# Regrouping copies in halves and one batch's value loads earlier, in a fused attention and gated feed-forward kernel

## The chip, the core and the metric

The kernel runs on one core of a Trainium2 chip. The metric is the device time of one execution in microseconds (us). Before the change the median of three runs is 412.39 us (412.38 to 412.73). The engines are named as in the profile: PE (TensorE), PEld (its weight loads), DVE (VectorE), ACT (ScalarE), POOL (GpSimd) and SP (SyncE). POOL and SP mainly issue DMAs here.

## The reference

Attention with a squared ReLU in place of the softmax, then a gated feed-forward layer:

```python
scores = q @ k.T / sqrt(64)
attn = maximum(scores, 0) ** 2 / 448
x = attn @ v                       # 8 batches, 12 heads, 448 rows, 64 columns
x = x by token                     # 3584 tokens of 768
out = (maximum(x @ w_gate, 0) * (x @ w_val)) @ w_out    # 768 -> 1536 -> 768
```

Inputs and output are float32; the kernel loads them into bf16 and accumulates in float32.

## The kernel before, in words

**Stages.** The eight batches are worked through as a pipeline. In turn b of the main loop (lines 740 to 785) PE computes the first projection of batch b-1, that is x @ w_gate and x @ w_val in twelve units of twelve steps (`gv_unit`, L304; ten units in turn 1), each step four 64x64 matmuls side by side. Between these steps stand the scores and value passes of batch b, and in turn 5 the first eleven of batch 6 as well. After turns 2 and 4 an `out_pair` (L357) computes the second projection of two batches, with sums and differences of blocks in place of some products. The last two batches have a first projection (`gv_pair`) and a second of the same kind at the end.

**Who does what for one tile.** A score tile goes into one of two PSUM pairs (L72). ACT takes the ReLU (r_sb, L234), DVE squares it into attn (L235). After seven tiles for each of three groups a value pass follows, whose result ACT (L268) and DVE (L269) copy to x, and DVE exchanges halves of partitions (L263). A unit of the first projection ends with a ReLU on ACT (g_sb, L322) and a product on DVE (hT, L323), which frees one of two accumulators for the unit after the next. For batches 6 and 7 the copies of the values are L278 to L281.

**Keys and queries.** The queries and keys of batches 2 to 7 are loaded into the same buffers kn and qn (`load_qk`, DMAs from POOL, L116). DVE regroups them by heads into kr and qr (`regroup`, L176, the copy at L179), and eight DMA transposes issued from SP (L186) bring them as kqT into one of two buffers. `hold(b)` (L676) is two tiny copies on POOL that read the last element of these transposes; POOL's queue, and so each load behind it, waits there.

**Order.** Every instruction is pinned to program order on its engine. The order comes from lists of events: an event is a unit, a step and a function, and `spread` (L690) calls it ahead of that step. `paced` places scores and value passes evenly over the turn. The regroupings, loads, holds and sums of weights are placed by hand in the lines 755 to 776. A place says where in each engine's queue the instructions stand; POOL and SP run ahead of PE as far as their waits allow.

**Weight sums.** `weight_sums(0)` and `(2)` (L343) are DVE operations on the rows of w_out, 128x2304 each (L347). They need the loads of w_out, which stand behind hold(2), and are used in the first `out_pair`.

**Stores.** `out_pair` issues its stores from POOL and SP (L411).

Of the kernel before, what the change touches and what calls it, by code (L numbers as in the profile page):

```python
# [16 lines left out]
def kernel(  # L17
# [22 lines left out]
    nc = tc.nc  # L40

    B, H, S, D = q.shape
# [25 lines left out]
    def pin(ins):  # L68
        return tc.keep_in_program_order(ins)
# [45 lines left out]
    def dma_in(o, i):  # L115
        pin(nc.gpsimd.dma_start(out=o, in_=i))  # L116
# [13 lines left out]
    def load_nat(dst, src, b, h0, h1):  # L130
        lo = src[b, h0:h1, 0:256, :].rearrange("h (j i) d -> j h i d", i=4)
        hi = src[b, h0:h1, 256:448, :].rearrange("h (j i) d -> j h i d", i=3)
        dma_in(dst[0:64, h0:h1, :, :], lo)
        dma_in(dst[64:128, h0:h1, 0:3, :], hi)

    def natural(b):

        return b if b < NB else 0

    def load_qk(b, h0=0, h1=H):  # L140
        load_nat(kn_b[natural(b)], k, b, h0, h1)
        load_nat(qn_b[natural(b)], q, b, h0, h1)

    def load_v(b):
        for c, p in HALVES:
            if b == 0:
                src = v[b].rearrange("(g c h) s d -> c h g s d", c=2, h=2)[c]
                dst = v_b[b % NB][p].rearrange("p (g h) i d -> p h g i d", h=2)
                parts = [(dst[:, h2], src[h2]) for h2 in range(2)]
            else:  # L150
                parts = [(v_b[b % NB][p], v[b, c * HP:c * HP + HP])]
            for dst, src in parts:
                dma_in(dst[:, :, 0:4, :], src[:, 0:256, :].rearrange("g (j i) d -> j g i d", i=4))
                dma_in(dst[:, :, 4:7, :], src[:, 256:448, :].rearrange("g (j i) d -> j g i d", i=3))
# [12 lines left out]
    def load_wo():  # L167
        for c in range(2):
            rows = moe_w_out[c * (d_ff // 2):(c + 1) * (d_ff // 2), :]
            dma_in(wo_sb[c], rows.rearrange("(kf p) m -> p kf m", p=128))  # L170
# [2 lines left out]

    T_b = [const.tile([128, 2, HP, S], BF16, name=f"kqT{i}") for i in range(NB)]

    def regroup(b, t):  # L176

        nat, grp = ((kn_b[natural(b)], kr), (qn_b[natural(b)], qr))[t]
        pin(nc.vector.tensor_copy(grp.rearrange("p i (h d) -> p i h d", d=D), nat.rearrange("p h i d -> p i h d")))  # L179

    def transpose_grouped(b, t):

        grp = (kr, qr)[t]
        for i in range(4):
            r = 128 if i < 3 else 64
            pin(nc.sync.dma_start_transpose(out=T_b[b % NB][:, t, :, i * 128:i * 128 + r], in_=grp[0:r, i, :]))  # L186

    def dma_transposes(b, t):
        regroup(b, t)
        transpose_grouped(b, t)  # L190

    def rotation(numbers):

# [97 lines left out]
    def quads(t):  # L291
        return [t[:, 2 * qd:2 * qd + 2, :] for qd in range(NQ)]

    def flat(t, n, c):

        names = " ".join("abcd"[:len(t.shape) - 1])
        return t.rearrange(f"p {names} -> p ({names})")[:, 0:n * c].rearrange("p (n c) -> p n c", c=c)

    def new_x(b):
        x = [xpool.tile([128, HP, S], BF16, name=f"x{n}") for n in range(2)]  # L300
        x_of[b] = [quads(t) for t in x]
        return x
# [40 lines left out]
    def weight_sums(n):  # L343

        o, a, b, op = ((T1, B12, B11, ALU.subtract), (B12, B22, B12, ALU.subtract),
                       (T2, B22, T1, ALU.subtract), (T4, B21, T2, ALU.subtract))[n]
        pin(nc.vector.tensor_tensor(o, a, b, op))  # L347
# [224 lines left out]
    def gv_units(b):  # L572
        b0 = b - b % 2
        if b == b0:
            hT_of[b0] = hpool.tile([128, KF, 2 * S], BF16, name="hT")
        return [gv_unit(b, mf, BEGUN, rotation((BEGUN_IN[mf],))) if b == 0 and mf < 2 else
                gv_unit(b, mf, BEGUN if mf == 0 else STRAIGHT, acc) for mf in range(KF)]
# [86 lines left out]
    def values_event(b, qd):  # L664
        return lambda: (values_by_parity if b >= B - 2 else values)(b, qd, sc_later())

    def transposes_event(b, qd):
        return lambda: transpose_quad(b, qd)
# [3 lines left out]
    def hold_unit(b, mf):  # L672

        pin(nc.gpsimd.tensor_copy(flag[:, 2:3], hT_of[b - b % 2][:, mf, b % 2 * S:b % 2 * S + 1]))

    def hold(b):  # L676

        for t in range(2):
            pin(nc.gpsimd.tensor_copy(flag[:, t:t + 1], T_b[b % NB][:, t, HP - 1, S - 1:S]))  # L679
# [23 lines left out]
        places = [at[int((i + 0.5) * len(at) / len(events))] for i in range(len(events))]  # L703
        return [(u, min(n, len(units[u]) - 4), e) for (u, n), e in zip(places, events)]

    def turned(b, *at):
        return [(u, n, lambda t=t: dma_transposes(b, t)) for t, (u, n) in enumerate(at)]

    def stream(b0, b1):

        e = []
        for b in range(b0, b1):
            for n in range(NT):
                if n % NC == 2 and (b, n) != (b0, 2):
                    vb, qd = (b, n // NC - 1) if n > NC else (b - 1, NQ - 1)
                    e.append((b, n, values_event(vb, qd), NC))
                e.append((b, n, scores_event(b, n), 1))
        return e

    def paced(units, first, behind, events):  # L720

        at = [(u, n) for u in range(len(units)) for n in range(len(units[u]))][first:behind]
        gaps = [{(1, 1): 1, (1, NC): 0.35, (NC, 1): 0.75}[a[3], b[3]] for a, b in zip(events, events[1:])]
        gap = len(at) / (sum(gaps) + 1)
        places, due = [], gap / 2
        for (*_, e, _), g in zip(events, gaps + [0]):
            u, n = at[int(due)]
            places.append((u, min(n, len(units[u]) - 4), e))
            due += g * gap
        return places  # L730
# [5 lines left out]
    units = gv_units(0)  # L736
# [3 lines left out]
    for b in range(1, B - 1):  # L740
        if b != B - 2:
            new_x(b)
        units = units[2:] if b == 1 else gv_units(b - 1)
        last = len(units) - 1
        if b < B - 3:
            first, behind = {1: (28, 109), 2: (40, 132)}.get(b, (0, 132))
            events = paced(units, first, behind, stream(b, b + 1))
            events.append((last, 8 if b == 1 else 5, values_event(b, NQ - 1)))
        else:
            todo = [e for e in attention if e[:2] <= ENDS[b]]  # L750
            del attention[:len(todo)]
            events = paced(units, 0, 144 if b == B - 3 else 132, todo)
            if b == B - 2:
                events.append((last, 5, values_event(B - 1, NQ - 1)))
        if b == 1:
            events += [(1, 2 + 4 * qd, transposes_event(1, qd)) for qd in range(NQ)]
            events += turned(2, (last - 3, 6), (last - 2, 6))
            events += [(last, 2, lambda: (hold(2), load_wo(), load_qk(3)))]
        elif b == 2:
            events += [(1, 1, lambda: load_v(3))]  # L760
            events += [(last - 2 + n, 6, lambda n=n: weight_sums(2 * n)) for n in range(2)]
            events += [(last - n, 9, lambda n=n: regroup(3, 1 - n)) for n in range(2)]
            events += [(last, 10, lambda: (transpose_grouped(3, 0), transpose_grouped(3, 1)))]
        elif b == 3:
            events += [(2, 1, lambda: (hold_unit(2, 1), hold(3), load_qk(4), load_v(4)))]
            events += turned(4, (6, 1), (7, 1)) + [(8, 2, lambda: (hold(4), load_qk(5)))]
        elif b == 4:
            events += turned(5, (3, 1), (4, 1)) + [(5, 2, lambda: (hold(5), load_qk(6), load_v(5)))]
        elif b == 5:
            events += turned(6, (1, 6), (2, 6)) + [(4, 1, lambda: (hold(6), load_v(6), load_qk(7)))]  # L770
            events += [(last - 3, 6, lambda: regroup(7, 0)), (last - 2, 3, lambda: regroup(7, 1))]
            events += [(last - 2, 6, lambda: (transpose_grouped(7, 0), transpose_grouped(7, 1)))]
            begun = flat(kn_b[1], 4, S)
            begun = x_of[B - 2] = [[begun[:, 2 * e:2 * e + 2, :]] for e in range(2)]
        elif b == 6:
            events += [(3, 1, lambda: (hold(7), load_v(7)))]
            new_x(b)
            for e in range(2):
                x_of[b][e][0] = begun[e][0]
            x_of[B - 1] = [quads(flat(t, HP, S)) for t in (kr, qr)]  # L780
        spread(units, events)
        if b == 2:
            out_pair(0, flat(kn_b[1], KH, S), [lambda: weight_sums(1), lambda: weight_sums(3)])
        elif b == 4:
            out_pair(2, flat(kn_b[1], KH, S))
# [45 lines left out]
```

## Time and profile before

| | |
|---|---|
| median of three runs | 412.39 us |
| the profiled execution | 411.69 us |
| its span | 409.9 us |
| mean TensorE clock granted | 0.993 |
| DMA moved | 44.17 MB |
| copies of L179 | 12, 0.95 to 0.96 us each |
| weight sums of L347 moved by the change | 2, 1.35 us each |

The span is what the profile covers of the execution. "Busy" counts the time in which an engine has an instruction under way; a matmul waiting in PE's own pipeline counts as busy. In timelines the bracket behind an instruction is the idle time of its engine just ahead of it and who ended it; "issue" means that the profile shows no releaser. The clock is the share of full TensorE speed that was granted.

### The profile page before, as it was taken

The numbers are of one execution on the slowest core, as the hardware profiler recorded it, in microseconds if no ns is written. First come the engines' busy times: TensorE is split into PE (matmuls) and PEld (weight loads), VectorE is DVE, ScalarE is ACT, GpSimd is POOL, SyncE is SP. The second block draws the span as 40 slices with busy tenths as digits, with TensorE's granted clock in tenths as the row PEclk, the third lists the DMA queues.
The fourth block names the chain that finished last, engine by engine and source line by source line (L and its number), as shares of the span: only waits on it lengthen the run. The fifth ranks groups of instructions, "written<-read, shape, count | busy, mean of one in ns | idle before, by whom it ended". The sixth has DMA issues, their size and how long they took to land.

```text
span 409.9 us, 16587 instructions
## 1 busy us (share of the span) xinstructions
PE 394.4 (96%) x7392; PEld 276.5 (67%) x7392; DVE 303.0 (74%) x520; ACT 244.1 (60%) x358; POOL 95.6 (23%) x164
## 2 busy tenths in 40 slices
PE   7899999999999999999999998899999999999994
PEld 4466666777776666666676686687677766777663
DVE  5885885589954786786833985888889969997651
ACT  4962984797334776877334888699973334444221
POOL 8834400610133502105034023020002230000230
PEclk9999999999999999999999999899999999999998
DMA  9999999699656994997927529960001350000144
GB/s 150 175 196 196 197 193 129 106 204 133 115 121 175 116 151 79 137 122 107 118 70 196 88 59 178 134 98 2 3 2 30 79 168 3 3 2 3 41 127 107
DMA packets 90984, 44.17 MB, mean 108 GB/s; under 512 B 55424, under 2 KB 89952, under 8 KB 90912
## 3 DMA queue, kind: packets, MB, share of 16 engines
q0 software_dynamic: 51136, 28.58, 49.0%
q1 hardware_dynamic: 39104, 13.99, 18.0%
q8 instruction: 58, 0.95, 1.0%
q10 hardware_dynamic: 672, 0.54, 0.6%
q14 instruction: 14, 0.11, 0.1%
HBM read 47.19 MB, written 11.01 MB: 142 GB/s over the span
## 4 chain that ended last, share of the span: by engine, by line
PE 69%; DMA 14%; DVE 7%; SPq 3%; issue 2%; POOL 2%; ACT 1%; DVEq 0%; POOLq 0%
PE ps L72 68%; DVE attn L235 4%; DMA wo<-in_moe_w_out_dram 4%; DMA qn<-in_q_dram 3%; DMA kn<-in_k_dram 3%; SPq L186 3%; DMA kqT<-qr 2%; DMA vn<-in_v_dram 2%; PE ps L210 1%; POOL kn L116 1%; DVE hT L323 1%; ACT r_sb L234 1%; POOL qn L116 1%; DVE x L642 1%; DVE kqT L211 0%
## 5 line engine op out<-in xcount | busy, mean ns | idle before, releaser
L72 PE MATMUL ps<-x,gv 64*64 64x448 bf16 x3552 | 204.6, 351 | 3.0 <-DVE hT L323 2.6
L72 PEld LDWEIGHTS <-gv 64*64 64x64 bf16 x4032 | 139.2, 107 | 58.3 <-issue 5.0
L234 ACT ACTIVATE r_sb<-ps 128x896 bf16<-128x896 f32 x167 | 147.8, 926 | 22.8 <-PE ps L72 19.4
L235 DVE TENSOR_TENSOR attn<-r_sb 128x896 bf16<-128x896 bf16 x167 | 102.3, 623 | 31.6 <-ACT r_sb L234 27.5
L72 PE MATMUL ps<-kqT 64*64 64x448 bf16 x672 | 67.8, 354 | 3.7 <-ACT r_sb L234 2.8
L72 PEld LDWEIGHTS <-hT 128*64 128x64 bf16 x1056 | 56.1, 110 | 20.9 <-issue 1.7
L411 POOL DMA_DIRECT2D out_dram<-attn x60 | 31.6, 531 | 163.5 <-DVE attn L401 131.9
L397 ACT ACTIVATE attn<-ps 128x384 f32<-128x384 f32 x64 | 28.9, 451 | 63.8 <-PE ps L72 63.2
L72 PE MATMUL ps<-wo,hT 128*64 128x384 bf16 (+1 forms) x720 | 53.9, 306 | 0.0
L323 DVE TENSOR_TENSOR hT<-ps,g_sb 128x448 bf16<-128x448 f32 x72 | 44.5, 619 | 9.3 <-ACT g_sb L322 8.8
L322 ACT ACTIVATE g_sb<-ps 128x448 bf16<-128x448 f32 x72 | 39.3, 547 | 18.5 <-PE ps L72 18.1
L401 DVE TENSOR_TENSOR attn<-ps,attn 128x384 f32<-128x384 f32 (+1 forms) x48 | 22.7, 503 | 32.1 <-ACT attn L397 18.1
L72 PEld LDWEIGHTS <-vn 64*64 64x64 bf16 (+1 forms) x840 | 30.8, 107 | 14.7 <-issue 3.9
L72 PEld LDWEIGHTS <-kqT 64*64 64x64 bf16 x672 | 27.2, 107 | 17.7 <-issue 7.5
L72 PE MATMUL ps<-attn,vn 64*64 64x448 bf16 x672 | 37.5, 350 | 1.0 <-issue 0.6
L515 ACT ACTIVATE kqT<-ps 128x896 f32<-128x896 f32 x18 | 16.5, 918 | 25.0 <-PE ps L72 25.0
L116 POOL DMA_DIRECT2D vn<-in_v_dram x36 | 23.7, 677 | 21.0 <-PE ps L72 5.8
L679 POOL COPY flag<-kqT 128x1 bf16<-128x1 bf16 x12 | 3.0, 252 | 101.6 <-DMA kqT<-kr 69.3
L72 PE MATMUL ps<-o_ring,hT 128*64 128x384 bf16 (+1 forms) x336 | 25.8, 306 | 0.1
L519 DVE TENSOR_TENSOR kqT<-ps,kqT 128x896 f32<-128x896 f32 x18 | 19.5, 1085 | 5.9 <-PE ps L72 4.2
L268 ACT ACTIVATE x<-ps 128x448 bf16<-128x448 f32 x15 | 8.2, 544 | 15.9 <-PE ps L72 15.9
L263 DVE COPY x<-x 64x896 bf16<-64x896 bf16 x36 | 14.4, 400 | 2.0
(104 smaller groups left out, 286.9 us busy)
## 6 DMA issues: line engine op xcount, KB each, us to landing
out_dram<-attn SPq DMA_DIRECT2D x48, 96.0 KB, 2.5
out_dram<-attn POOLq DMA_DIRECT2D x46, 96.0 KB, 2.3
kn<-in_k_dram POOLq DMA_DIRECT2D x7, 384.0 KB, 7.0
qn<-in_q_dram POOLq DMA_DIRECT2D x7, 384.0 KB, 9.2
vn<-in_v_dram POOLq DMA_DIRECT2D x14, 192.0 KB, 9.0
gv<-in_moe_w_gate_dram POOLq DMA_DIRECT2D x6, 384.0 KB, 11.3
gv<-in_moe_w_val_dram POOLq DMA_DIRECT2D x6, 384.0 KB, 10.9
wo<-in_moe_w_out_dram POOLq DMA_DIRECT2D x2, 1152.0 KB, 12.4
```

The lines of the kernel that those rows point to most:

```text
L72: pin(nc.tensor.matmul(o, lhsT=l, rhs=r, start=start, stop=stop, skip_group_check=True))
L116: pin(nc.gpsimd.dma_start(out=o, in_=i))
L234: pin(nc.scalar.activation(r, src, AF.Relu))
L235: pin(nc.vector.tensor_tensor(dst, r, r, ALU.mult))
L263: pin(nc.vector.tensor_copy(x1[p], x0[other]))
L322: pin(nc.scalar.activation(g_sb, o[0], AF.Relu, scale=float(out_scale)))
L323: pin(nc.vector.tensor_tensor(hT[:, mf, col:col + S], o[1], g_sb, ALU.mult))
L397: pin(nc.scalar.activation(out_of(t, r, c), bank(P, t), AF.Copy))
L401: pin(nc.vector.tensor_tensor(o, bank(Q, t), o, ALU.add))
L411: pin(engines[c].dma_start(out=rows[:, c0:c1, :], in_=src))
L515: pin(nc.scalar.activation(held(n, j), both(PQ[n][0]), AF.Copy))
L519: pin(nc.vector.tensor_tensor(k, both(PQ[n][1]), k, ALU.add))
```

## The change

`regroup` and `transpose_grouped` take a half h and treat two of the four groups of rows, so that each regrouping is two copies of 128x1536. `turned` places four pieces, keys' halves and queries' halves, each half with its two transposes, the second half five steps behind the first. `step` adds steps across the border of a unit. In the turns:

- turn 1 (batch 2): one step later, in halves.
- turn 2: the two weight sums three and two units sooner; batch 3's regroupings in halves at steps 3 and 8 of the last two units, keys first (they stood at step 9 of the last two units).
- turns 3 and 4 (batches 4 and 5): in halves from the same places; the holds and loads behind them two steps later in the lists.
- turn 4, new: the loads of batch 6's values at step 9 of the last unit, ahead of the second `out_pair`.
- turn 5: these loads no longer stand between hold(6) and the loads of batch 7's keys and queries; batch 7's regroupings move from unit 8, step 6 (keys) and unit 9, step 3 (queries) to units 9 and 10, steps 6 and 11; their transposes stand with them and no longer together at unit 9, step 6.

```diff
-    def regroup(b, t):
+    def regroup(b, t, h):
 
         nat, grp = ((kn_b[natural(b)], kr), (qn_b[natural(b)], qr))[t]
-        pin(nc.vector.tensor_copy(grp.rearrange("p i (h d) -> p i h d", d=D), nat.rearrange("p h i d -> p i h d")))
-
-    def transpose_grouped(b, t):
+        i = slice(2 * h, 2 * h + 2)
+        pin(nc.vector.tensor_copy(grp.rearrange("p i (h d) -> p i h d", d=D)[:, i],
+                                  nat.rearrange("p h i d -> p i h d")[:, i]))
+
+    def transpose_grouped(b, t, h):
 
         grp = (kr, qr)[t]
-        for i in range(4):
+        for i in (2 * h, 2 * h + 1):
...
-    def turned(b, *at):
-        return [(u, n, lambda t=t: dma_transposes(b, t)) for t, (u, n) in enumerate(at)]
+    def step(units, u, n, k):
+        at = len(units[0]) * u + n + k
+        return at // len(units[0]), at % len(units[0])
+
+    def turned(b, units, *at):
+
+        def piece(t, h):
+            regroup(b, t, h)
+            transpose_grouped(b, t, h)
+        return [(*step(units, u, n, 5 * h), lambda t=t, h=h: piece(t, h)) for t, (u, n) in enumerate(at) for h in range(2)]
...
-            events += turned(2, (last - 3, 6), (last - 2, 6))
+            events += turned(2, units, (last - 3, 7), (last - 2, 7))
...
-            events += [(last - 2 + n, 6, lambda n=n: weight_sums(2 * n)) for n in range(2)]
-            events += [(last - n, 9, lambda n=n: regroup(3, 1 - n)) for n in range(2)]
-            events += [(last, 10, lambda: (transpose_grouped(3, 0), transpose_grouped(3, 1)))]
+            events += [(last - 5 + 2 * n, 6, lambda n=n: weight_sums(2 * n)) for n in range(2)]
+            events += [(last - 1 + t, 3 + 5 * h, lambda t=t, h=h: regroup(3, t, h)) for t in range(2) for h in range(2)]
+            events += [(last, 10, lambda: [transpose_grouped(3, t, h) for t in range(2) for h in range(2)])]
...
-            events += turned(4, (6, 1), (7, 1)) + [(8, 2, lambda: (hold(4), load_qk(5)))]
+            events += turned(4, units, (6, 1), (7, 1)) + [(8, 4, lambda: (hold(4), load_qk(5)))]
...
-            events += turned(5, (3, 1), (4, 1)) + [(5, 2, lambda: (hold(5), load_qk(6), load_v(5)))]
+            events += turned(5, units, (3, 1), (4, 1)) + [(5, 4, lambda: (hold(5), load_qk(6), load_v(5))), (last, 9, lambda: load_v(6))]
...
-            events += turned(6, (1, 6), (2, 6)) + [(4, 1, lambda: (hold(6), load_v(6), load_qk(7)))]
-            events += [(last - 3, 6, lambda: regroup(7, 0)), (last - 2, 3, lambda: regroup(7, 1))]
-            events += [(last - 2, 6, lambda: (transpose_grouped(7, 0), transpose_grouped(7, 1)))]
+            events += turned(6, units, (1, 6), (2, 6)) + [(4, 1, lambda: (hold(6), load_qk(7)))]
+            events += turned(7, units, (last - 2, 6), (last - 1, 6))
```

More of the change, by code (lines that the diff above doesn't have):

```diff
@@ L174 @@
     T_b = [const.tile([128, 2, HP, S], BF16, name=f"kqT{i}") for i in range(NB)]
-    def regroup(b, t):
+    def regroup(b, t, h):
         nat, grp = ((kn_b[natural(b)], kr), (qn_b[natural(b)], qr))[t]
-        pin(nc.vector.tensor_copy(grp.rearrange("p i (h d) -> p i h d", d=D), nat.rearrange("p h i d -> p i h d")))
-    def transpose_grouped(b, t):
+        i = slice(2 * h, 2 * h + 2)
+        pin(nc.vector.tensor_copy(grp.rearrange("p i (h d) -> p i h d", d=D)[:, i],
+                                  nat.rearrange("p h i d -> p i h d")[:, i]))
+    def transpose_grouped(b, t, h):
         grp = (kr, qr)[t]
-        for i in range(4):
+        for i in (2 * h, 2 * h + 1):
             r = 128 if i < 3 else 64
             pin(nc.sync.dma_start_transpose(out=T_b[b % NB][:, t, :, i * 128:i * 128 + r], in_=grp[0:r, i, :]))
-    def dma_transposes(b, t):
-        regroup(b, t)
-        transpose_grouped(b, t)
     def rotation(numbers):
```

## The prediction

> **What bounds the kernel now.** I read the page's busy times first, then the idle pieces of PE in order of time, then windows of one microsecond around the largest piece, and last the DVE and POOL timelines there, to see who held whom.
>
> ```profile
> PE 394.4 (96%) x7392; PEld 276.5 (67%) x7392; DVE 303.0 (74%) x520; ACT 244.1 (60%) x358; POOL 95.6 (23%) x164
> ...
> PEclk9999999999999999999999999899999999999998
> ```
>
> PE is busy 96% of 409.9 us, and the change leaves its instructions alone: their order on PE, ACT and SP is the same in both programs, and only DVE's and POOL's change. So all that can be gained is time in which PE stands idle or runs at less than its full clock. The idle pieces from 25 us on are 0.24 (53.7), 0.63 (59.0), 0.57 (65.6), 0.27 (101.8), 2.61 (257.3), 0.46 (292.9) and 0.28 (396.7): 5.1 us. The only slice with a lower clock ahead of the end is the one around 257.
>
> The one-microsecond windows there (columns: stretch, length, PE, PEld, DVE, ACT and POOL busy with counts, PE clock, DMA share, GB/s):
>
> ```profile
> 253.00:254.00 1.00, 1.00 (x31) 0.80 (x24) 0.00 (x0) 0.96 (x2) 0.00 (x0) 1.00 1.52 184
> ...
> 255.00:256.00 1.00, 0.00 (x0) 0.00 (x0) 0.77 (x1) 0.47 (x2) 0.00 (x0) 1.00 1.45 199
> ...
> 257.00:258.00 1.00, 0.68 (x12) 0.51 (x15) 0.80 (x2) 0.00 (x0) 0.00 (x0) 0.76 1.72 191
> 258.00:259.00 1.00, 1.00 (x17) 0.62 (x13) 0.15 (x1) 0.10 (x1) 0.00 (x0) 0.50 0.83 129
> 259.00:260.00 1.00, 1.00 (x16) 0.71 (x12) 1.00 (x2) 0.81 (x1) 0.00 (x0) 0.50 0.85 177
> 260.00:261.00 1.00, 1.00 (x16) 0.66 (x12) 1.00 (x3) 0.24 (x1) 0.00 (x0) 0.53 0.87 197
> 261.00:262.00 1.00, 1.00 (x28) 0.81 (x23) 1.00 (x3) 0.98 (x2) 0.00 (x0) 1.00 0.40 97
> ```
>
> DVE falls silent first (253 to 254), then PE (255 to 256); when PE returns its clock is 0.50 for about 3.4 us, with 16 matmuls counted per microsecond instead of 28. Who made DVE wait is in the timeline (start, length, instruction, idle before):
>
> ```profile
> 243.34 0.19 POOL L679 COPY flag<-kqT 128x1 bf16<-128x1 bf16 x1 [8.10 <-DMA kqT<-qr]
> ...
> 243.89 2.68 POOL L116 DMA_DIRECT2D vn<-in_v_dram  x4 [0.37 <-issue]
> ...
> 246.52 1.55 POOL L116 DMA_DIRECT2D kn<-in_k_dram  x2
> ...
> 248.00 1.58 POOL L116 DMA_DIRECT2D qn<-in_q_dram  x2
> ...
> 251.16 0.79 DVE L263 COPY x<-x 64x896 bf16<-64x896 bf16 x2
> ...
> 255.23 0.96 DVE L179 COPY kr<-kn 128x3072 bf16<-128x3072 bf16 x1 [3.28 <-issue]
> ...
> 256.65 0.62 DVE L323 TENSOR_TENSOR hT<-ps,g_sb 128x448 bf16<-128x448 f32 x1
> ...
> 257.32 1.17 PE L72 MATMUL ps<-x,gv 64*64 64x448 bf16 x10 [2.61 <-DVE hT L323]
> ```
>
> DVE stands at the regrouping of batch 7's keys (L179), a copy of what the keys' loads bring (the view of the tile kn names it as the one who waited, 3.3 us). These were issued at 246.5 and 247.3, behind the four loads of batch 6's values (2.68 us of POOL), and land 7.0 and 7.9 us later, at 255.2. Queued behind that copy on DVE stands hT L323, which frees a PSUM bank for PE.
>
> **Part by part.**
>
> *Batch 6's values ahead, batch 7's regroupings later.* The four value loads go to POOL's queue ahead of the stores of the second projection. There they wait for PE's last reading of the buffer, batch 4's last value pass, which ends near 196.7. Behind them queue POOL's stores, the first at 204.65 and waiting for DVE then, so 8 us cover four issues of 2.7 us. The transfers before them end at 200.9 (GB/s falls from 143 to 12), and 0.69 MB at about 190 GB/s is 3.6 us: done by 204.5. Cost nothing; uncovered, it would be a store a few us later, and the buffers that the stores free are wanted only 20 us on.
>
> In the old place the keys' loads then go out at 243.9 and 244.7. For batch 5, loaded with no values ahead, keys landed 5.6 and 6.5 us and queries 7.7 and 8.5 us after their issue. So keys land by 251.2, queries (last issue about 246.2) by 254.7. The regroupings move from unit 8, step 6 and unit 9, step 3 to units 9 and 10, steps 6 and 11. Units 8 and 9 end at 251.8 and 254.9 (their g_sb), so DVE reaches the first key half near 254, the first query half near 257: 2.8 and 2.3 us to spare. Even with the loads where they were (255.2, 258.7) DVE would wait a microsecond or two, not 3.3. So the stall goes: 2.61 us idle, and of the clock 0.24 + 0.50 + 0.50 + 0.47 = 1.71. **-4.3 us.** As a check, 250 to 270 shows 330 matmuls and 225 to 245 shows 424; the missing 94 at 20/424 us each are 4.4 us.
>
> The clock may be weighed against a rule of the skill. The trace shows 0.50 right behind a gap of 2.61 us, and full clock 3.4 us after PE resumed. The Trainium skill, "TensorE: Matmul & The Clock Gate" (Part 1), says that the clock halves after at least one idle window of about 3.4 us and returns after about 3.4 us of work. The return agrees; the fall does not, as the gap here is shorter. By the letter of that rule the gap would not be the cause of the 1.71 us and only 2.61 would be gained here; the sum goes by the trace.
>
> *Batch 7's transposes.* They stay in SP's queue, eight in a row, 5.19 + 6.08 us now. Started at 254.5 instead of 256.3, they end near 266 and land by 270 (DMA kqT<-qr took 3.3 to 4.4 us). The first score of batch 7 has 42 others since batch 5's start ahead of it; it stands at 277.60 now and would stand at 273. Three us are left; values 7, held behind them, land near 276 and are wanted at 288.0 - 4.6 = 283.4.
>
> *Halves.* No half is in the trace. From the 64x896 copy (0.39 us) and the 128x3072 copy (0.955) the slope is 0.26 ns per element with 0.16 fixed, so a half of 1536 is about 0.56; the bounds are 0.48 (half, no fixed part) and 0.955. Twelve pairs add 12 x 0.16 = 1.9 us to a DVE that is busy 303 of 409.9, on no path except where PE waits for DVE. One such place: batch 2. Keys land at 55.24, the copy runs 55.37 to 56.33, and PE waits 0.63 us for x L269, which ends at 59.0. Now one attn is done ahead of the copy; behind it come half, attn, hT, half, attn, x instead of whole, attn, attn, hT, attn, x. One attn less (0.54 us per start) and 0.16 more: x ends about 0.4 earlier. **-0.4.** SP's first two transposes start about 0.45 us earlier and cover the wait for the second half, here and for batches 4 to 6; the weights' loads behind hold(2) come no later.
>
> *Two weight sums sooner.* They leave 96.4 and 99.8 for the places behind an L263 in unit 6 (about 87.1) and behind the first attn past unit 7's hT (about 92.1). The weights landed at 84.2 and 90.4, so 1.7 us are left for the second. Their gain: attn L235 at 101.11, for which PE waits 0.27 us, comes sooner. **-0.3.** Their cost: 1.26 us of DVE each in a stretch where DVE idles about 1.1 us between 88 and 93. Followed instruction by instruction, x L269 then ends at 95.6 instead of 94.9, and the score at 95.45 needs that bank: **+0.2** (from 0 to 0.8).
>
> *Batch 7's regroupings beside work.* In the stall they cost nothing of their own; now 4 x 0.56 us stand in units 9 and 10, which last 3.1 us each with about 2.3 us of DVE work. DVE falls about a microsecond behind. PE has two accumulators, so a lag below a unit is covered, but the value copies L279 follow: **+0.2** (from 0 to 1.5, were all lag beyond 0.75 us to reach PE).
>
> *The rest.* The loads of batches 5 and 6 move two steps later, behind hold(4) and hold(5), which wait for SP anyway: 0. The 0.57 at 65.6 has no releaser and the 0.46 at 292.9 comes from ACT's order, which is the same: 0.
>
> Sum: -4.3 - 0.4 - 0.3 + 0.2 + 0.2 = **-4.6 us**. The profiled execution took 411.69 us (span 409.9 and 1.8 around it), so 407.1 for its like; the median of the runs is 0.70 above it, so **407.8**.
>
> **Rivals.** (a) *DVE or ACT becomes the bound behind the stall.* Against: 225 to 245 has DVE 18.0 and ACT 17.9 of 20 us busy and PE still 19.9. For: after the stall DVE is full until 268. If 1 to 2.5 us come back as small waits: 408.8 to 410.3.
>
> (b) *The half clock is not the gap's doing* and is met elsewhere: only 2.61 + 0.3 is gained, 409.5. Against it: no other slice is low before the end. This is the result that the Trainium skill's rule above would have.
>
> (c) *Nothing moves*: hold(6) ends so much later that the queries still land 3 us behind DVE. Against: its transposes are SP-bound, 228.5 to 240.0, and start sooner. About 412.
>
> (d) *Slower: batch 7's transposes come late.* Four transposes took 8.74 us beside loads at 56.5, against 5.2 here. Eight at that pace from 255 end at 272.5 and land at 276.5; PE, which arrives at 273.0, would idle 3.5 us and lose 1.7 by the clock, all that was gained: 413.0, and 414 with one more microsecond. It decides from a landing past 273. Against: hold(7) keeps the loads behind them, and the value loads that shared the DMA are gone.
>
> (e) *More is gained*: in the runs without profile, 0.7 us longer, the stall may be longer too. 406.4 to 406.9.
>
> **Numbers.** Forecast (407.0 to 408.7): 0.65. (a) 0.13, (b) 0.06, (c) 0.05, (d) 0.06, (e) 0.05. A measurement of this kernel can tell about 0.2%, 0.8 us, from no change. Faster: 0.65 + 0.13 + 0.06 + 0.05 = 0.89; same 0.05; slower 0.06. The range leaves out (c), (d) and the tail of (a): 406.6 to 410.0.
>
> **What would show it.** Right: no idle piece over 0.5 us between 230 and 270, PEclk 1.00 there, the keys' loads 2.7 us behind the flag gone to 0.5; 59.0 and 101.8 shrunk; the first POOL store within 0.5 us of where it was. Wrong: a regrouping with an idle time "issue" over 1 us ahead of it; score waits on ACT or DVE spread over 255 to 275; PE waiting at batch 7's first score; the second weight sum waiting for wo.

## The result, and the profile after

The changed kernel takes 407.66 us (median of 4 runs, 406.69 to 408.46), the kernel before 412.38 us beside it (4 runs, 411.17 to 412.73): the ratio is 0.989 [0.9858, 0.9922], faster by 4.7 us. The prediction was 407.8. All ratios are worked out from the runs within 1.5% of the fastest of their kernel (414.94 and 413.21, named below, are not) and so differ a little from those of the medians. The profiled execution took 406.69 us, with a span of 404.9. Line numbers are now two or three lower, except the regrouping copy (L179, now L180); L277 is the DVE half of the value copies, L279 before.

The page after, busy times and granted clock:

```profile
PE 393.0 (97%) x7392; PEld 276.3 (68%) x7392; DVE 303.9 (75%) x532; ACT 244.3 (60%) x358; POOL 96.0 (24%) x164
...
PEclk9999999999999999999999999999999999999999
```

The count of matmuls is the same, PE is busy 1.4 us less, and the 8 in the clock's row is gone. DVE has twelve more instructions (the halves) and 0.9 us more work.

The windows around the old stall (columns as before):

```profile
250.00:270.00 20.00, 19.37 (x408) 15.24 (x404) 18.22 (x34) 18.00 (x26) 2.97 (x6) 1.00 0.41 75
...
259.00:260.00 1.00, 0.37 (x9) 0.14 (x7) 0.97 (x3) 0.57 (x1) 0.00 (x0) 1.00 0.60 93
```

The same 20 us now hold 408 matmuls, where there were 330, and the clock is 1.00 throughout. One gap is left, in 259 to 260. The timeline shows both why the old one is gone and where the new one comes from:

```profile
239.15 0.19 POOL L677 COPY flag<-kqT 128x1 bf16<-128x1 bf16 x1 [5.82 <-DMA kqT<-qr]
239.71 1.64 POOL L116 DMA_DIRECT2D kn<-in_k_dram  x2 [0.37 <-issue]
241.34 1.51 POOL L116 DMA_DIRECT2D qn<-in_q_dram  x2
...
253.42 0.55 DVE L180 COPY kr<-kn 128x1536 bf16<-128x1536 bf16 x1
...
255.96 0.55 DVE L180 COPY qr<-qn 128x1536 bf16<-128x1536 bf16 x1
...
258.50 1.27 DVE L277 TENSOR_SCALAR kn<-ps 64x448 bf16<-64x448 f32 x2
259.82 0.38 PE L72 MATMUL ps<-kqT 64*64 64x448 bf16 x2 [0.63 <-DVE kn L277]
```

The keys' loads stand right behind the flag, the tiny copy of hold(6) that waits for the transposes (0.56 us later; it was 3.18). Keys land by about 246.5 and queries by 250.6 (the loads' own times from issue to landing are 5.2 to 8.5 us), so all four half copies (the second halves at 254.43 and 256.96) run without a bracket: DVE no longer waits. But four of them now stand ahead of the value copies L277, whose PSUM pair the next score needs, and PE waits 0.63 us for these.

The moved value loads, on POOL:

```profile
194.76 1.98 POOL L116 DMA_DIRECT2D vn<-in_v_dram  x3 [2.36 <-PE ps L72]
197.43 0.66 POOL L116 DMA_DIRECT2D vn<-in_v_dram  x1 [0.68 <-DMA qn<-in_q_dram]
202.98 4.23 POOL L409 DMA_DIRECT2D out_dram<-attn  x8 [4.89 <-DVE attn L399]
```

They wait for PE's last reading of the buffer and are issued by 198.1. POOL then waits another 4.89 us for what it is to store, so they hold up nothing.

**Where the 5.0 us of the span went.** PE reaches its landmarks sooner by: first projection 0.31, first `out_pair` 1.69, second 1.68, batch 7's first score 5.13, last product 5.13. The start-up (0.31) is the same program in both kernels. Turns 1 and 2 bring 1.38: the pieces at 59.0 (0.63), 65.6 (0.57) and 101.8 (0.27) are gone. Turns 3 and 4, which also got halves, bring nothing. Turn 5 brings 3.45: the 4.3 of the stall, less the new wait of 0.63 and 0.24 that I did not place. Whatever follows brings nothing.

### The profile page after: what moved, and what is told of

It reads as the page before. It is cut to its first block, busy times and chain, and to the rows that moved or that the text cites. A ratio compares the mean times of both kernels' runs of the same rounds, so it can differ in the third digit from the quotient of the medians.

```text
span 404.9 us, 16604 instructions
## 1 busy us (share of the span) xinstructions
PE 393.0 (97%) x7392; PEld 276.3 (68%) x7392; DVE 303.9 (75%) x532; ACT 244.3 (60%) x358; POOL 96.0 (24%) x164
## 4 chain that ended last, share of the span: by engine, by line
PE 79%; DVE 7%; DMA 5%; ACT 3%; issue 2%; SPq 2%; POOL 0%; DVEq 0%; ACTq 0%; POOLq 0%
PE ps L72 78%; DVE attn L233 4%; DMA kn<-in_k_dram 3%; ACT r_sb L232 3%; SPq L409 2%; DMA qn<-in_q_dram 1%; PE ps L208 1%; DMA out_dram<-attn 1%; DVE x L640 1%; DVE attn L399 0%; DVE kqT L209 0%; DVE hT L321 0%; ACT g_sb L320 0%; DVE kr L180 0%; DVE qr L180 0%
```

## The experiments

My theory: the four value loads ahead of the keys' loads make DVE wait at the regrouping, PE starves behind it, and the half clock follows from PE's gap; taking the loads out of the way gives nearly the whole gain. Rivals: the gain comes from the later place of the regroupings, from the halves or from the weight sums; or the half clock has nothing to do with the gap. The runs were made on three chips; the kernel before took 411.39, 412.57 and 412.65 us there, and each ratio is against the kernel before on the same chip.

**The value loads alone** (kernel before, whole copies, all else in its old place):

```diff
-            events += turned(5, (3, 1), (4, 1)) + [(5, 2, lambda: (hold(5), load_qk(6), load_v(5)))]
+            events += turned(5, (3, 1), (4, 1)) + [(5, 2, lambda: (hold(5), load_qk(6), load_v(5))), (last, 9, lambda: load_v(6))]
...
-            events += turned(6, (1, 6), (2, 6)) + [(4, 1, lambda: (hold(6), load_v(6), load_qk(7)))]
+            events += turned(6, (1, 6), (2, 6)) + [(4, 1, lambda: (hold(6), load_qk(7)))]
```

> The kernel before with one edit: batch 6's value loads stand ahead of the second out_pair's stores; everything else, the regroupings of batch 7 too, as before. My theory (the stall at 257 is batch 7's keys landing late, and the value loads ahead of them are what makes them late): keys land about 5 to 7 us after their issue near 243.5, that is by 250.5, DVE reaches their regrouping near 252.0, so no idle time ahead of it and no stretch at clock 0.50: 4.0 to 4.3 us less than before, ratio about 0.990. Rival A (the later place of the regroupings is what does it): the stall stays, under 1 us is gained. Rival B (the half clock is not the gap's doing): 2.6 us are gained and a stretch at 0.50 stays.

Measured 407.43 (406.54 to 407.8), ratio 0.9898 [0.9862, 0.9934]. Its timeline:

```profile
242.22 1.74 POOL L116 DMA_DIRECT2D kn<-in_k_dram  x2 [0.31 <-DVE attn L235]
...
252.68 0.96 DVE L179 COPY kr<-kn 128x3072 bf16<-128x3072 bf16 x1
...
255.16 0.95 DVE L179 COPY qr<-qn 128x3072 bf16<-128x3072 bf16 x1
```

and its window over the old stall:

```profile
250.00:270.00 20.00, 20.00 (x424) 15.59 (x420) 18.30 (x33) 17.83 (x26) 1.47 (x4) 1.00 0.48 89
```

Both copies run without a wait and PE stands still for nothing in 20 us: 424 matmuls, as many as in the undisturbed 225 to 245 of before. This one edit gives the whole gain that these measurements can tell. The pieces at 59.08 (0.63) and 101.87 (0.27) are still in its profile, as they should be.

**The later place alone** (loads in the old order, whole copies):

```diff
-            events += [(last - 3, 6, lambda: regroup(7, 0)), (last - 2, 3, lambda: regroup(7, 1))]
-            events += [(last - 2, 6, lambda: (transpose_grouped(7, 0), transpose_grouped(7, 1)))]
+            events += turned(7, (last - 2, 6), (last - 1, 6))
```

> The kernel before with one edit: batch 7's regroupings and their transposes stand in units 9 and 10, step 6 (whole copies), the loads as before. My theory as put on record: even then DVE would wait a microsecond or two, not 3.3; keys land at 255.2, DVE is there near 254; queries land at 258.7, DVE is there near 257.5. PE has an accumulator to spare, so PE idles 0 to 1 us: 3.0 to 4.3 us less than before, ratio 0.990 to 0.993. Rival A (only the loads' order counts, the wait just moves with the place): within 1 us of before.

Measured 410.53 (407.15 to 414.94), ratio 0.9962 [0.993, 0.9995]: 1.6 us by the ratio, not 3.0 or more. The expectation failed. The profiled execution took 407.15, the least of its runs. No copy waits there, and PE idles only for the value copies L279 (0.49 us at 260.07). Two more profiles of the same kernel follow.

> The kernel with only the later place of batch 7's regroupings, once more for a second profile: its twelve times went from 407.15 to 414.94 and its first profile, at 407.15, showed no wait. My theory: its gain hangs on when the loads land, which differs between executions; in a longer execution DVE idles ahead of a copy of kr or qr near 255, with PE idle behind it. Rival: no wait there in a longer execution either, so that the spread comes from elsewhere.

> The kernel with only the later place of batch 7's regroupings, for a third profile. My theory: in a longer execution DVE idles ahead of a copy of kr or qr near 255. Rival: it does not, and the spread comes from elsewhere.

The first of them (410.9 us) has DVE waiting 1.26 us for the queries and PE idle 1.85 us at 263.52, with the clock at 1.00. The second (413.67 us), its timeline:

```profile
261.13 0.96 DVE L179 COPY qr<-qn 128x3072 bf16<-128x3072 bf16 x1 [1.40 <-issue]
...
263.61 1.27 DVE L279 TENSOR_SCALAR kn<-ps 64x448 bf16<-64x448 f32 x2
...
264.93 0.38 PE L72 MATMUL ps<-kqT 64*64 64x448 bf16 x2 [1.98 <-DVE kn L279]
```

and its windows behind that gap:

```profile
266.00:267.00 1.00, 1.00 (x16) 0.72 (x12) 0.93 (x3) 0.70 (x2) 0.00 (x0) 0.50 0.48 105
...
270.00:271.00 1.00, 1.00 (x31) 0.76 (x23) 0.63 (x1) 1.00 (x3) 0.38 (x1) 1.00 0.01 0
```

DVE's wait has shrunk to 1.3 or 1.4 us, but PE's gap hardly has: the place only hands it from hT to the value copies L279, and no second buffer covers those. In this execution the flag came at 245.63, after POOL had waited 8.01 us for the queries' transposes. In the execution of 407.15 it came at 239.82, after 5.58 us. The queries landed near 255.3, 259.7 and 261.1 in the three profiles, and DVE waited for them 0, 1.26 and 1.40 us. With the later place alone, what is gained hangs on when the loads land.

**The kernel before, a second profile**, to learn whether the stall of the first is typical.

> The kernel before itself, for a second profile. My theory: DVE waits for batch 7's keys or queries again and PE idles 1.5 to 3 us near 257, but the sizes differ; where no single gap reaches about 2.6 us the clock stays at 1.00. If the stall is not there, the gain hangs on chance.

410.47 us: DVE waits 2.21 us at 254.25 (keys) and 1.04 at 257.85 (queries), and PE is idle 1.54 and 1.10 us, both at hT:

```profile
256.33 0.76 PE L72 MATMUL ps<-x,gv 64*64 64x448 bf16 x10 [1.54 <-DVE hT L323]
...
260.46 0.38 PE L72 MATMUL ps<-x,gv 64*64 64x448 bf16 x2 [1.10 <-DVE hT L323]
```

The clock stays at 1.00. So the stall is there again at 2.64 us of idle PE, in two pieces; the 1.71 us of lost clock are not.

**The values behind the keys and queries** (kernel before, loads still in turn 5):

```diff
-            events += turned(6, (1, 6), (2, 6)) + [(4, 1, lambda: (hold(6), load_v(6), load_qk(7)))]
+            events += turned(6, (1, 6), (2, 6)) + [(4, 1, lambda: (hold(6), load_qk(7), load_v(6)))]
```

> The kernel before with one edit: batch 6's value loads stand in the same event, but behind batch 7's key and query loads instead of ahead of them. It tells the order on POOL's queue from the earlier place ahead of the stores. My theory (the keys are late because the values are ahead of them): keys land 5 to 6 us after their issue and no copy of batch 7 waits; the values now land last, where the queries landed before, near 257.5, and PE's first value pass of batch 6 would stand near 257.5 without the stall, so 0 to 1.5 us are lost there: 2.8 to 4.3 us less than before. Rival (only the place ahead of the stores, with the DMA queue empty at hold(6), brings the gain): under 2 us less.

Measured 408.89 (406.86 to 413.21), ratio 0.993 [0.9884, 0.9976]: 2.9 us, within the expectation, but the interval (1.0 to 4.8 us) leaves room for the rival's "under 2 us", so the profile has to decide. The profiled execution took 407.57 us; its timeline:

```profile
243.72 1.54 POOL L116 DMA_DIRECT2D kn<-in_k_dram  x2 [0.37 <-DVE hT L323]
245.23 1.52 POOL L116 DMA_DIRECT2D qn<-in_q_dram  x2
246.70 2.69 POOL L116 DMA_DIRECT2D vn<-in_v_dram  x4
...
252.18 0.96 DVE L179 COPY kr<-kn 128x3072 bf16<-128x3072 bf16 x1
...
254.66 0.95 DVE L179 COPY qr<-qn 128x3072 bf16<-128x3072 bf16 x1
```

The same bytes at nearly the same time, in another order, and the stall is gone, though the flag came at 243.16, as late as in the first profile of before (243.34). So it is the order behind the values that held DVE, and the place ahead of the stores is one way to change it. The order costs twice: with the four value loads ahead, the keys' loads go out 2.7 us later, and they land 6.4 to 9.0 us after their issue in the seven profiles with that order, 4.9 to 7.0 here. The place ahead of the stores may be the steadier way: the runs in the ratio here reach 411.8, those of the loads alone end at 407.8; but those are six runs, on another chip. The values now land late (8.9 to 9.9 us after issue), and batch 6's value pass at 257.55 took 1.81 us where it takes 1.52 with the loads alone. That this is what spreads the runs was not shown.

**Halves alone** (the changed kernel, with the loads, batch 7's places and the weight sums put back as before):

```diff
-            events += [(last - 5 + 2 * n, 6, lambda n=n: weight_sums(2 * n)) for n in range(2)]
+            events += [(last - 2 + n, 6, lambda n=n: weight_sums(2 * n)) for n in range(2)]
...
-            events += turned(5, units, (3, 1), (4, 1)) + [(5, 4, lambda: (hold(5), load_qk(6), load_v(5))), (last, 9, lambda: load_v(6))]
+            events += turned(5, units, (3, 1), (4, 1)) + [(5, 4, lambda: (hold(5), load_qk(6), load_v(5)))]
...
-            events += turned(6, units, (1, 6), (2, 6)) + [(4, 1, lambda: (hold(6), load_qk(7)))]
-            events += turned(7, units, (last - 2, 6), (last - 1, 6))
+            events += turned(6, units, (1, 6), (2, 6)) + [(4, 1, lambda: (hold(6), load_v(6), load_qk(7)))]
+            events += [(last - 3, 6, lambda: [regroup(7, 0, h) for h in range(2)]),
+                       (last - 2, 3, lambda: [regroup(7, 1, h) for h in range(2)])]
+            events += [(last - 2, 6, lambda: [transpose_grouped(7, t, h) for t in range(2) for h in range(2)])]
```

> The kernel before with the regroupings of batches 2 to 6 in halves at the changed kernel's places; batch 7's two halves back to back in the old place, the value loads and the weight sums as before. My theory: the idle piece at 59.0 (0.63 us) goes, as in the changed kernel, and the stall at 257 stays at 2.6 us with its slow clock: 0.4 to 0.7 us less, 0.9985. The piece of 0.57 us at 65.6 that went too with the change has no releaser in the profile: if it goes here, it hangs on the halves of batch 2, else it is chance. Rival: the halves' extra time on DVE (1.9 us in all) shows as waits, 0 to 1 us more than before.

411.1 (408.61 to 413.83), ratio 0.9988 [0.996, 1.0017]: no difference that can be told. In its profile the stall is back, smaller than expected (1.62 us at 261.17, clock 1.00). The piece at 59 did not go, and one old wait has grown:

```profile
56.28 0.56 DVE L180 COPY kr<-kn 128x1536 bf16<-128x1536 bf16 x1 [0.46 <-DMA kn<-in_k_dram]
...
59.50 0.38 PE L72 MATMUL ps<-kqT 64*64 64x448 bf16 x2 [0.55 <-DVE x L267]
...
99.74 0.55 DVE L180 COPY kr<-kn 128x1536 bf16<-128x1536 bf16 x1
...
100.75 1.35 DVE L345 TENSOR_TENSOR o_ring<-wo,qn 128x2304 bf16<-128x2304 bf16 x1
102.01 0.62 DVE L233 TENSOR_TENSOR attn<-r_sb 128x896 bf16<-128x896 bf16 x1
```

At 59, batch 2's keys landed late and DVE waited 0.46 us for them, so 0.55 us of PE's idle time are left with halves: this part of the expectation failed. The piece at 65.6 is there too (0.56 at 66.04), so the halves do not remove it. Batch 3's first half copy now stands at step 3, ahead of the weight sum that still has its late place, and PE waits 0.73 us for the attn behind both, where it was 0.27. The two edits belong together.

**Weight sums alone** (kernel before):

```diff
-            events += [(last - 2 + n, 6, lambda n=n: weight_sums(2 * n)) for n in range(2)]
+            events += [(last - 5 + 2 * n, 6, lambda n=n: weight_sums(2 * n)) for n in range(2)]
```

> The kernel before with one edit: the two weight sums three and two units sooner. My theory: the idle piece of 0.27 us at 101.8 goes and no wait of PE comes in its place near 95, as the changed kernel showed none: 0.2 to 0.3 us less, which a measurement can hardly tell from no change; the pieces at 59.0 and 257 stay. Rival (the price of 0.2 on record, a score waiting for x L269 near 95): a piece of about 0.2 us there, nothing gained.

412.13 (408.88 to 414.49), ratio 1.0009 [0.9976, 1.0042]: no difference that can be told, as 0.3 us is below what these runs resolve. In the profile the piece at 101.8 is gone and no score waits near 95. Batch 2's keys landed late here (DVE waits 2.12 us for them), and the piece at 59 has grown to two, 1.05 at 59.08 and 0.63 at 61.22. In the stall PE is idle 0.79 us up to 257.88 and 1.99 us up to 262.90, 2.78 in all, and the clock stays at 1.00; the last section comes back to that.

**The changed kernel with whole copies** (each at its first half's place, batch 3's too, all else as changed):

```diff
-        i = slice(2 * h, 2 * h + 2)
-        pin(nc.vector.tensor_copy(grp.rearrange("p i (h d) -> p i h d", d=D)[:, i],
-                                  nat.rearrange("p h i d -> p i h d")[:, i]))
+        if h == 0:
+            pin(nc.vector.tensor_copy(grp.rearrange("p i (h d) -> p i h d", d=D), nat.rearrange("p h i d -> p i h d")))
...
-        return [(*step(units, u, n, 5 * h), lambda t=t, h=h: piece(t, h)) for t, (u, n) in enumerate(at) for h in range(2)]
+        return [(*step(units, u, n, 0), lambda t=t, h=h: piece(t, h)) for t, (u, n) in enumerate(at) for h in range(2)]
```

> The changed kernel with whole copies: each regrouping is one copy of 128x3072 at the place of its first half, its four transposes behind it; loads, places and weight sums as changed. My theory: the stall stays gone (the loads do that), what is lost against the changed kernel is at most the 0.6 us of the piece at 59.0, and some of it comes back since DVE does 1.9 us less: 0 to 0.6 us slower than the changed kernel. Rival (the halves carry a good part of the gain): over 1 us slower.

407.86 (407.27 to 409.94), ratio 0.9892 [0.9856, 0.9929]. **The changed kernel again**, on the same chip:

> The changed kernel itself, for a narrower interval on the same chip as the three others and for a second profile. My theory: as measured first, ratio 0.988 to 0.990, with the new piece of PE idle time near 260 behind the value copies (0.63 us in the first profile, DVE kn L277) there again, since it comes from DVE's order; the piece of 0.57 us at 65.6 may or may not be there, since it came and went in kernels that differ nowhere near it. If the 0.63 is not there, it was chance too.

408.94 (406.8 to 410.32), ratio 0.9902 [0.9871, 0.9934], where 0.988 to 0.990 was expected. Whole copies are as fast. At 58.55 their profile has a piece of 0.33 us, where before had 0.63 and the changed kernel has none. That does not split the gain between halves and place, since the piece hangs on when batch 2's keys land: it is 0.37 in the second profile of before and 0.55 with halves alone. The repeat has the new wait again:

```profile
261.37 0.38 PE L72 MATMUL ps<-kqT 64*64 64x448 bf16 x2 [0.62 <-DVE kn L277]
```

So 0.62 to 0.63 us belong to the order on DVE, not to one execution. Whole copies have it too (0.58 at 261.84, and 0.49 with the later place alone): it comes with the place, not with the halves. The 0.57 us piece at 65.6 is the contrary: in the repeat it is back at 64.87 (0.54, "issue"), so its absence after was chance.

**Batch 7's regroupings one unit sooner** (changed kernel), to get rid of that wait:

```diff
-            events += turned(7, units, (last - 2, 6), (last - 1, 6))
+            events += turned(7, units, (last - 3, 6), (last - 2, 6))
```

> The changed kernel with batch 7's four pieces one unit sooner (units 8 and 9, steps 6 and 11). Keys and queries landed by 246.5 and 250.6 in the changed kernel's profile, so neither waits there; the pieces leave the stretch ahead of the value copies of batch 6. My theory (the wait of 0.63 us near 260 is DVE lag from four halves packed into units 9 and 10): it shrinks to under 0.2, 0.3 to 0.6 us less than the changed kernel. Rival (the wait comes from the value copies' own place): it stays, no difference.

407.24 (406.35 to 409.25), ratio 0.9873 [0.9835, 0.991]. The window of the profile:

```profile
250.00:270.00 20.00, 19.98 (x416) 15.90 (x412) 18.15 (x35) 17.82 (x26) 0.35 (x2) 1.00 0.77 124
```

The wait near 260 is gone, and PE has no idle piece of 0.2 us or more from 135 to 290, though the flag came as late as 245.26. This is the lowest median of all, faster than the kernel before; the intervals do not tell it from the changed kernel.

**Gaps made on purpose** (changed kernel, with 16 to 24 DVE writes of a tile that nothing reads, in turns 2 to 5; it adds work and leaves none out):

```diff
+        late = {2: 16, 3: 20, 4: 24, 5: 20}.get(b)
+        if late:
+            events.append((4, 6, lambda: [pin(nc.vector.memset(blank, 0.0)) for _ in range(late)]))
```

> The changed kernel with DVE held up on purpose in turns 2 to 5: 16, 20, 24 and 20 memsets of a tile that nothing reads again, at unit 4, step 6. Each should make PE idle for some time, none of it over a missing load. My theory (the clock falls because PE stood idle, and only past some length): behind gaps under about 2 us, as with the 1.62 and 1.99 us met in two runs so far, the clock stays at 1.00; behind a gap of 2.6 us or more it is 0.50 for about 3.4 us, as at 257 before the change. Rival (the half clock there had another cause): gaps of 2.6 us and more here leave the clock at 1.00.

One run, 435.08 us. PE's gaps are 3.65, 4.86, 6.93 and 4.05 us, and a stretch at 0.50 stands behind each. The second of them:

```profile
148.00:149.00 1.00, 0.00 (x0) 0.00 (x0) 0.73 (x3) 0.00 (x0) 0.00 (x0) 1.00 1.49 194
...
150.00:151.00 1.00, 0.00 (x0) 0.00 (x0) 0.66 (x4) 0.00 (x0) 0.00 (x0) 0.50 1.49 193
...
153.00:154.00 1.00, 1.00 (x17) 0.59 (x12) 1.00 (x3) 0.26 (x1) 0.00 (x0) 0.50 0.00 0
...
157.00:158.00 1.00, 1.00 (x29) 0.69 (x21) 0.01 (x1) 0.86 (x1) 0.00 (x0) 1.00 0.08 16
```

PE stopped near 146.8; the clock falls while it still stands, and is back 4.8 us after it resumes at 151.67. So the gap makes the half clock, wherever in the program it is put.

## Why the prediction was right, point by point

- **The stall, -4.3.** Right in cause and, for the profiled pair, in size: 2.61 idle and 1.71 of clock are both gone, and the loads alone give a ratio of 0.9898. But 4.3 was one execution's stall. In the second profile of before the idle part is the same (2.64), with weight sums alone it is 2.78, and in both the clock's part is nothing. Sized over executions it lies between 2.6 and 4.3, and the medians do not contradict that: 4.0 for the loads alone, 3.6 and 4.7 for the whole change.
- **Batch 7's regroupings beside work, +0.2 (0 to 1.5).** Mis-sized: 0.63 and 0.62 in two profiles. The way was named, the value copies. What the estimate missed is that two accumulators cover the lag of hT but nothing covers L277.
- **Halves, -0.4.** The piece of 0.63 at 59.0 is gone in both profiles of the changed kernel, but 0.55 of it is left with halves alone, where the keys landed later: the estimate took their landing as fixed. A half took 0.55 us (0.56 expected). In time halves show nothing alone (0.9988 [0.996, 1.0017]).
- **Weight sums, -0.3 and +0.2.** The 0.27 at 101.8 is gone; the price did not appear, no wait near 95. The sums ran at 85.64 and 90.70, neither waiting for wo. In time they show nothing alone either.
- **The rest, 0.** The 0.57 at 65.6 and the start-up's 0.31 are gone from the profile after, by chance. Without these 0.88 the profile's -5.0 is -4.1, against the -4.6 predicted. The new wait cost 0.43 more than put down, but the piece at 59.0 gave 0.23 more and the price of the sums 0.2, which cancels it; the 0.5 us that are missing lie in small pieces that I did not place (0.24 of them in turn 5).
- **The total.** 407.66 against 407.8 is closer than these terms deserve, so part of it is luck: in the profiled pair chance added 0.88 us, and a stall with its clock part, which some four in ten executions have (last section), had been taken for typical. Measured again on another chip the changed kernel took 408.94, 3.6 us below the kernel before there, and the intervals are about 0.3% to each side, not the 0.2% that I had thought could be told.
- **Margins.** Keys and queries landed 7 and 5 us ahead of DVE, not 2.8 and 2.3: the flag came at 239.15, since the queries' transposes landed 5.8 us behind the keys' (8.1 before). That is not the change's doing; two profiles of one kernel above have 5.8 and 8.0.
- **The first store within 0.5 us of its place.** It came at 202.98 instead of 204.65, with PE, which is 1.68 us sooner there.
- **"Even with the loads where they were DVE would wait a microsecond or two".** DVE did (1.26, 1.40); the 3.0 us or more that I then expected of the place alone was wrong, as PE's gap stayed near 1.9 us.

**The rivals.** (a) DVE and ACT are full from 250 to 270 (18.2 and 18.0) and give back 0.63, below the 1 to 2.5 asked for. (c) falls with the loads alone. (d) was never near: the last transposes landed at 267.34, batch 7's first score came at 272.47, 5.1 us later. (b) falls in its first half, since gaps made on purpose bring the half clock. The Trainium skill's rule in "TensorE: Matmul & The Clock Gate" (Part 1), an idle window of about 3.4 us, does not tell when if it is read as an unbroken gap: gaps of 2.61 (before) and 1.98 us were followed by 0.50, gaps of 1.99, 1.85, 1.62 and 1.54 were not. As the length of a window it agrees, 3.41 us here; the last section shows from the profiles what decides. The clock was back 3.6 us after PE resumed; 3.4 is how long it stood at 0.50. (e) needs 406.4 to 406.9, and neither median of the changed kernel (407.66, 408.94) is there.

## What to carry to other kernels

When an engine idles "<-issue" at a copy of loaded data, look at what stands ahead of that load in the issuing queue: loads that are wanted later can be put behind it or into an earlier slot of the same queue, and that was worth 0.7% and 1.0% here. Moving the consumer later instead trades the wait for one at the next result without a second buffer. Size such a stall from two or three executions, the half clock behind it above all, before it goes into a sum.

## What the hardware showed beyond that

- **The clock is set every 3.41 us, by how long PE idled since it was last set.** In the run with gaps the clock fell at 84.80, 149.65, 194.02, 265.70 and, behind the end of PE's work, 432.96. These falls stand 19, 13, 21 and 49 times 3.413 us apart, and each stretch at 0.50 between them lasted that once or twice. In the kernel before, the falls at 257.52 and 407.70 stand 44 times apart. So the fall at the end of a profile shows where the borders lie in all of it, and PE's idle time can be counted from border to border:

| profile | border to border | PE idle | clock behind it |
|---|---|---|---|
| before | 254.11 to 257.52 | 2.61 | 0.50 |
| later place, third profile | 262.31 to 265.72 | 1.98 | 0.50 |
| gaps | 149.65 to 153.06 | 2.02 | 0.50 |
| changed kernel, its end | 397.93 to 401.35 | 1.91 | 1.00 |
| later place, second profile | 260.00 to 263.41 | 1.74 | 1.00 |
| weight sums alone | 258.60 to 262.02 | 1.11 | 1.00 |
| weight sums alone | 262.02 to 265.43 | 0.88 | 1.00 |

Two rows of the view of windows, the third profile of the later place and then the first row of the weight sums (PE's busy time stands behind the length):

```profile
262.31:265.72 3.41, 1.43 (x33) 0.80 (x28) 3.32 (x8) 1.37 (x3) 0.28 (x1) 1.00 0.62 140
258.60:262.02 3.42, 2.31 (x52) 1.55 (x41) 1.74 (x3) 2.42 (x4) 0.00 (x0) 1.00 0.80 131
```

In the fourteen profiles no such stretch with 1.98 us idle or more is followed by the full clock, and none with 1.91 or less by 0.50. That is why a gap of 1.98 us cost the clock and one of 1.99 did not: a border at 262.02 cut the second in two. The borders lie elsewhere in each execution, so the same gap costs the clock in one and not in the next.
- **How often the stall cost the clock.** In the thirteen profiles without added gaps the mean clock of the execution is 0.993 for the two with a stretch at 0.50 ahead of the end, and 0.996 to 1.000 for the others. At 0.994 or below are 23 of the 56 runs of the kernel before that stand beside the experiments, and none of the 31 runs of kernels with the value loads moved ahead of the stores (lowest 0.996).
- **The spread is smaller without the race for the loads.** On its three chips the kernel before ran from 409.1 to 414.1, 410.3 to 415.1 and 408.5 to 414.2 us (runs in the ratios). With the value loads moved the runs lie from 406.5 to 407.8 (loads alone), 406.8 to 410.3 (changed kernel again) and 406.4 to 409.3 (one unit sooner). POOL waited 8.1 and 5.7 us for the same four transposes in two profiles of before, and 5.6, 5.8 and 8.0 in three of the later place. That this is what spreads the runs is not shown.
- **Other idle pieces of PE come and go** between executions of kernels that do not differ there, at 38 to 40 us (0.2 to 0.9) and near 65 us (0.35 to 1.06), both without a releaser: their cause is open. Pieces of 0.27 to 0.67 us near 133 are in seven of the fourteen profiles; DVE waits 3.7 to 4.1 us for a store there, where it waits 1.8 in before. They are as large as two of the terms of the sum.
